# Attention as one written list of parts per pair, products with v in four visits, and the short chunk's scores in fp32 quarters

## The chip, the cores and the metric

One NeuronCore of a Trainium2 chip runs the whole program. The metric is device time in microseconds (us), the median of several runs; less is better. The engines are named as in the profile: PE (TensorE, with PEld its weight loads), DVE (VectorE), ACT (ScalarE), POOL (GpSimd) and SP, which issues the transfers.

## What is computed

Three layers, one behind the other. The attention has 4 batches of 8 heads, 576 tokens and a head size of 64:

```python
scores = scale * np.matmul(q, k.transpose(0, 1, 3, 2))
thresh = np.max(scores, axis=-1, keepdims=True) - tau
scores = np.where(scores >= thresh, scores, -1000000000.0)
scores = scores - np.max(scores, axis=-1, keepdims=True)
attn = np.exp(scores)
attn = attn / (np.sum(attn, axis=-1, keepdims=True) + 1e-09)
return np.matmul(attn, v).astype(np.float32)
```

Its output, 2304 tokens of 512 values, goes through an MLP (512 to 2048 to 512, with h * tanh(softplus(h)) between), and that through a soft mixture of 8 experts with 4 slots each. Everything is fp32; only the attention is touched by the change, apart from the layout of the inputs.

## The kernel before, in words

Two heads of a batch make a **pair**; there are NPR = 16 pairs. A pair's queries are cut into **chunks** of 128 score rows: four chunks of 128 queries for each head, and one short chunk that holds the last 64 queries of both heads, nine in all. The line `chunks += ...` (L283) gives their order: queries 0 to 127 of head 0, then of head 1, and so on, the short chunk last.

Inputs are split so that matmuls in the reduced format fp32r (one matmul instruction) keep fp32's accuracy. k is scaled by -1/8 into `ks` (fp32); `kb` holds its high part on partitions 0 to 63 and the low part on 64 to 127 (`prep_k`, L220). q is split into `Q1` (high part, on both halves) and `Q2` (low part), L233. This is POOL's work, one pair ahead; the first pair is split by ACT, DVE and POOL (`prep_first`, L239). A product of two fp32 tiles, as those with v, shows as two matmul instructions in the profile.

A chunk passes through these steps:

- **S** (`emit_S`, L293): scores into a PSUM tile `s` of two banks, 288 keys in each; 4 matmuls. For the short chunk `Q1` and `Q2` have 64 zero columns, so that each head's 64 queries fill their own half of 128 rows: 10 matmuls of 128 columns by 288, 224 or 64.
- **E** (`emit_E`, L311): DVE takes the minimum `nm` (L316; the scores are negated), ACT the exponential `e` (L317). Then `th` = `nm` + tau (L323, DVE).
- **P** (`emit_P`, L326): DVE keeps `e` where the score is within the threshold, and sums the row (L339).
- **T** (`emit_T`, L345): PE transposes four blocks of 128 keys into a bank `tp`, and ACT copies them to `pT` (L362, L364; a copy by ACT is line L93 in the profile).
- **R** (`emit_R`, L366 on, and `evac_R`): the last 64 keys of both heads of a chunk are transposed together into the unused columns of an `s` tile and copied to `pTr`.
- **V** (`emit_V`, L389): the product with v, heads side by side in two 64-column halves of the array, in five steps over keys (four of 128 and the rest). The queries go in two halves, of 256 and of 320, each into one bank `tp`, which stays open over two visits: three steps, then two (`PV`, L36). ACT copies the result to `xT`.

PSUM has three `s` tiles (`ps_s`, six banks) and two `tp` banks (`ps_t`). A tile is written again only when its readers are done: S of a chunk waits for P of the chunk three before.

The order on every engine is the order in which the code emits. The loop at L558 goes over chunks i and emits in each turn: a visit of V if one is due, R, S of chunk i, another V, T of chunk i-3 (`T_LAG`), minimum and exponential of chunk i, P of chunk i-1, the threshold of chunk i, and then the side work by j, the place in the pair: k of the next pair at j = 1 and 3, q at 5 and 7, loads of the pair after next at 4 and 8, steps of the conversion of early weights (`conv_w` with fine; `CONV`, L39), the norm of the batch before (`norm_c`, L444, POOL, at 5), and in pairs 12 to 15 the split of the first MLP block's x (`x_hi` on ACT, `x_lo` on POOL, L463, at 6). Nine more turns drain the last pair, with the first MLP products (`mm1`, L490 to L492) between.

What the prediction speaks of further: the first MLP stage's second product (L654 to L656), the transposed MLP (L749 to L751) and the logits (L801, four 32-column tiles of the array), none of which is changed.

Of the kernel before, what the change touches and what calls it, by code (L numbers as in the profile page):

```python
# [18 lines left out]
NP = H // 2  # L19
# [50 lines left out]
def kernel(  # L70
    ctx: ExitStack,
    tc: tile.TileContext,
    q: bass.AP,
    k: bass.AP,
# [55 lines left out]
    Q1 = [p1.tile([128, 2 * S + 64], F32R, name=f"Q1_{i}") for i in range(2)]  # L130
    Q2 = [p1.tile([128, 2 * S + 64], F32R, name=f"Q2_{i}") for i in range(2)]
# [73 lines left out]
    def load_first():  # L205
        kt = raw[0, "k"] = p1.tile([128, 2, S], F32, name="kr")
        qt = raw[0, "q"] = p1.tile([128, 2, S], F32, name="qr")
        for h in range(2):
            sp.dma_start(out=kt[:, h], in_=k[0, 0, :, h])
            sp.dma_start(out=qt[:, h], in_=q[0, 0, :, h])  # L210
# [18 lines left out]
    def q_parts(n, h):  # L229
        o = slice(0, S) if h == 0 else slice(S + 64, 2 * S + 64)  # L230
        return Q1[n % 2][:, o], Q2[n % 2][:, o]

# [6 lines left out]
    def prep_first():  # L239
# [4 lines left out]
        def part(x, h, c):  # L244
            return x[:, slice(S + 64 + c.start, S + 64 + c.stop) if h else c]
# [5 lines left out]
        def low_k(h):  # L251
            dve.tensor_tensor(out=kb[64:, h], in0=ks[64:, h], in1=kb[64:, h].bitcast(F32), op=ALU.subtract)
# [21 lines left out]
        low_q(1, z, pool)  # L274
# [7 lines left out]
    for n in range(NPR):  # L282
        chunks += [(n, c, h) for c in range(4) for h in range(2)] + [(n, 4, 0)]  # L283
# [3 lines left out]
    def q_off(c, h):  # L287
        return 128 * c + (S + 128 if h else 0)
# [3 lines left out]

    def emit_S(i):  # L293
        n, c, h = chunks[i]
        q1, q2 = Q1[n % 2], Q2[n % 2]
        kb = KB[n][0]
        s = st[i]["s"]
        whole = ((0, 0, SH, 0), (1, 0, SH, SH))
        if c < 4:
            plan = [(t, q_off(c, h), h, whole) for t in (q1, q2)]  # L300
        else:
            rot = ((0, 0, SH, 64), (1, 0, SH - 64, SH + 64), (1, SH - 64, SH, 0))
            plan = [(q1, 512, 0, whole), (q2, 512, 0, whole), (q1, S, 1, rot), (q2, S, 1, rot)]
        for j, (t, o, hh, parts) in enumerate(plan):
            for f, a, z, ko in parts:
                pe.matmul(  # L306
                    s[:, f, a:z], lhsT=t[:, o:o + 128], rhs=kb[:, hh, ko:ko + z - a],
                    start=(j == 0), stop=(j == len(plan) - 1 and z == SH),
                )

    def emit_E(i):  # L311
        d = st[i]
        s = d["s"][:, :, :SH]
        nm = p1.tile([128, 1], F32, name="nm", bufs=4)
        e = p2.tile([128, 2, SH], F32, name="e", bufs=3)
        dve.tensor_reduce(out=nm, in_=s, axis=AX.XY, op=ALU.min)  # L316
        act.activation(out=e, in_=s, func=ACTF.Exp, bias=nm[:, 0:1], scale=-1.0)  # L317
        d["nm"], d["e"] = nm, e

    def emit_th(i):  # L320
        d = st[i]
        th = p1.tile([128, 1], F32, name="th", bufs=4)
        dve.tensor_scalar(out=th, in0=d["nm"], scalar1=tau_eff[:, 0:1], scalar2=None, op0=ALU.add)  # L323
        d["th"] = th
# [19 lines left out]

    def emit_T(i):  # L345
        n, c, h = chunks[i]
        half = 0 if c < 2 else 1
        if (n, half) not in pT:
            w = 256 if half == 0 else 320
            pT[n, half] = (  # L350
                p1.tile([128, 4, 2, w], F32, name=f"pT{half}"),
                p1.tile([128, w], F32, name=f"pTr{half}"),
            )
        t = pT[n, half][0]
        p = st[i]["p"]
        ps = ps_t.tile([128, 512], F32, name="tp").rearrange("p (a b) -> p a b", a=4)
        for kc in range(4):
            ko = 128 * kc + (64 if h else 0)
            pe.transpose(ps[:, kc], p[:, ko:ko + 128], ident)  # L359
        if c < 4:  # L360
            o = (c % 2) * 128
            copy_act(t[:, :, h, o:o + 128], ps)  # L362
        else:
            copy_act(t[:, :, :, 256:320], ps.rearrange("p a (h q) -> p a h q", h=2))  # L364
# [3 lines left out]
    def emit_R(n, part, i):  # L368


        ps = rest[n, part] = st[i]["s"][:, :, SH:SH + 128]
        if part == 2:
            pe.transpose(ps[:, 0], pr[:, 512:640], ident)
            return
        for j in range(2):
            pe.transpose(ps[:, j], pp[n, 2 * part + j][:, 512:640], ident)

    def evac_R(n, part):
        ps = rest.pop((n, part))
        if part < 2:  # L380
            copy_act(pT[n, part][1][:, :256].rearrange("p (a b) -> p a b", a=2), ps)
        else:
            tr = pT[n, 1][1]
            copy_act(tr[:64, 256:320], ps[:64, 0, :64])
            copy_act(tr[64:, 256:320], ps[:64, 0, 64:])
# [3 lines left out]
    def emit_V(n, half, kcs):  # L389


        b, hp = divmod(n, NP)
        w = 256 if half == 0 else 320
        t, tr = pT[n, half]
# [9 lines left out]
        if kcs[-1] < 4:  # L404
            return
        for blk, x0, p0, ln in spans(b * S + 256 * half, w):
            copy_act(xT[blk][:, hp, x0:x0 + ln], pv[:, p0:p0 + ln])

    def pv_at(i, z):

        n, k = divmod(3 * i + z, 27)
        for half, plan in enumerate(PV):
            for back in range(2):
                if k + 27 * back in plan and 0 <= n - back < NPR:
                    emit_V(n - back, half, plan[k + 27 * back])
# [7 lines left out]
    def norm_b(b, i):  # L423
        o = SH if i < NCH else 0
        ps = st[i]["s"][:36, 0, o:o + 128]
        pe.transpose(ps, rinv[b], ident)
        return lambda: norm_out(b, ps)

    def norm_out(b, ps):
# [78 lines left out]
    with tc.manual_schedule():  # L508
        dve.tensor_copy(out=idr, in_=ident)
        sp.dma_start(out=tau_sb, in_=tau)  # L510
        load_first()
        load_v(0)
        load_k(1)
        load_q(1)
# [4 lines left out]
        zz = const.tile([128, 64], F32, name="zz")  # L519
        dve.memset(zz, 0.0)  # L520
        for t in Q1 + Q2:
            dve.tensor_copy(out=t[:, S:S + 64], in_=zz)
# [4 lines left out]
        prep_first()  # L527
# [30 lines left out]
        for i in range(NCH + 9):  # L558
            n, j = divmod(i, 9)
            live = i < NCH  # L560
            if live or j in R_AT[1:]:
                st[i] = {"s": ps_s.tile([128, 2, 512], F32, name="s")}
            R = None
            pv_at(i, 0)
            if n < NPR and j == R_AT[0]:
                R = (n, 0, i)
            if n >= 1 and j in R_AT[1:]:
# [812 lines left out]
```

## Time and profile before

| | |
|---|---|
| runs | 741.07, 739.01 and 739.6 us, median 739.6 |
| profiled execution, span from the first to the last instruction | 737.1 us |
| the profiled execution's own time | not given apart from its span; the median of the runs is 2.5 us above that span |
| mean granted clock of TensorE | 0.992 of 2.4 GHz |
| attention with its drain | about the first 282 us |
| instructions | 12728 |

The page is one profiled execution. A busy share is an average over stages with other limits, so each stage is read from its own windows. In the chain of waits a piece is time in which the end of the program hung on that line; where pieces of PE follow each other without a gap, PE alone sets the pace. A matmul's own duration is longer than its share of that chain, since matmuls overlap.

### The profile page before, as it was taken

To read this page: it belongs to the slowest core of one execution; us is meant where nothing else is said; L and a number is where in the kernel's file an instruction comes from. 1 tells how busy PE (TensorE), PEld (TensorE's weight loads), DVE (VectorE), ACT (ScalarE), POOL (GpSimd) and SP (SyncE) were. 2 spreads that over 40 slices of the span, in tenths; PEclk is the share of its full clock that TensorE was granted. 3 is DMA by queue.
4 is the path that set the end of the run, shared out by engine and by line. 5 is a ranking of instruction groups with operands and counts; after the bars stand their busy time and mean duration, and the time that the engine had idled before them with its cause. 6 is when DMAs were issued, how large, how long until landed. Compare 5 with 4: busy or idle time off the path is not lost.

```text
span 737.1 us, 12728 instructions
## 1 busy us (share of the span) xinstructions
PE 717.8 (97%) x4625; PEld 587.9 (80%) x4625; DVE 527.1 (72%) x1018; ACT 453.2 (61%) x880; POOL 391.3 (53%) x395
## 2 busy tenths in 40 slices
PE   7999999999999999999999899999999999999995
PEld 6777777777777778999899888878898888888443
DVE  7999999999998855656977756578866446754413
ACT  6887787787777875445554645566656556545213
POOL 5766677667768642333746644566755544544000
PEclk8999999999999999999999999999999999999998
DMA  7422533453313023334311000000006111359798
GB/s 242 148 84 86 187 100 99 145 167 109 99 62 132 23 75 115 114 123 149 128 58 45 20 1 1 1 1 0 1 12 238 58 59 58 124 215 364 259 397 305
DMA packets 45678, 84.85 MB, mean 115 GB/s; under 512 B 6048, under 2 KB 21040, under 8 KB 45616
## 3 DMA queue, kind: packets, MB, share of 16 engines
q1 hardware_dynamic: 45344, 83.88, 33.6%
q8 instruction: 36, 0.59, 0.3%
q14 instruction: 26, 0.21, 0.1%
q10 hardware_dynamic: 272, 0.16, 0.1%
HBM read 79.23 MB, written 4.79 MB: 114 GB/s over the span
## 4 chain that ended last, share of the span: by engine, by line
PE 86%; ACT 5%; DVE 4%; issue 2%; POOL 2%; DMA 1%; SPq 0%; ACTq 0%
PE tp L403 11%; PE s L306 10%; PE s L654 9%; PE s L656 8%; PE s L655 8%; PE tp L359 8%; PE tp L749 5%; PE tp L751 5%; PE tp L750 5%; PE tp L490 3%; PE tp L492 3%; PE tp L491 3%; PE hp L1202 2%; PE so L1234 2%; ACT big L93 1%
## 5 line engine op out<-in xcount | busy, mean ns | idle before, releaser
L306 PE MATMUL s<-kb,Q 128*128 128x288 f32 (+2 forms) x672 | 125.4, 314 | 4.1 <-POOL Q L237 1.2
L473 POOL TENSOR_TENSOR wo<-wr,wo 128x512 fp32r<-128x512 f32 x48 | 68.3, 1424 | 99.9 <-ACT wo L93 86.5
L316 DVE TENSOR_REDUCE nm<-s 128x1 f32<-128x576 f32 x144 | 108.1, 751 | 17.8 <-PE s L306 15.4
L654 PE MATMUL s<-wo,gg 128*128 128x512 f32 x288 | 115.4, 401 | 0.7 <-DVE big L664 0.7
L656 PE MATMUL s<-wo,gg 128*128 128x512 f32 x288 | 113.6, 394 | 0.0
L655 PE MATMUL s<-wo,gg 128*128 128x512 f32 x288 | 113.4, 394 | 0.0
L93 ACT ACTIVATE pT<-tp 128x512 f32<-128x512 f32 x144 | 86.6, 601 | 38.8 <-PE tp L359 36.0
L317 ACT ACTIVATE e<-s,nm 128x576 f32<-128x576 f32 x144 | 106.7, 741 | 5.7 <-DVE nm L316 5.5
L306 PEld LDWEIGHTS s<-kb,Q 128*128 128x128 f32 x672 | 95.3, 192 | 18.4 <-issue 6.5
L339 DVE SCALAR_TENSOR_TENSOR pab<-s,th,e 128x576 f32<-128x576 f32 x128 | 103.5, 808 | 0.3 <-ACT pTr L93 0.3
L359 PE MATMUL tp<-ident,pab 128*128 128x128 f32 x512 | 79.2, 278 | 0.0
L403 PE MATMUL tp<-pT,vt 128*64 128x320 f32 (+1 forms) x512 | 76.0, 418 | 0.4 <-ACT pT L93 0.4
L739 POOL TENSOR_TENSOR wi<-wr,wi 128x256 fp32r<-128x256 f32 x48 | 47.2, 985 | 40.0 <-ACT wi L93 40.0
L760 ACT ACTIVATE hs<-hs 128x384 f32<-128x384 f32 x64 | 33.4, 522 | 56.5 <-DVE hs L1038 35.8
L359 PEld LDWEIGHTS tp<-ident,pab 128*128 128x128 f32 x512 | 61.1, 141 | 7.8 <-ACT e L317 4.9
L739 POOL TENSOR_TENSOR wi<-ev,wi 128x256 fp32r<-128x256 f32 x64 | 52.5, 831 | 23.8 <-ACT wi L93 23.8
L656 PEld LDWEIGHTS s<-wo,gg 128*128 128x128 f32 x288 | 54.1, 188 | 12.5
L654 PEld LDWEIGHTS s<-wo,gg 128*128 128x128 f32 x288 | 54.2, 188 | 9.8 <-issue 1.8
L655 PEld LDWEIGHTS s<-wo,gg 128*128 128x128 f32 x288 | 54.4, 189 | 7.4 <-POOL wo L473 0.4
L763 DVE TENSOR_TENSOR gg<-hs,gg 128x384 fp32r<-128x384 f32 x64 | 54.5, 852 | 7.6 <-ACT gg L93 7.6
L93 ACT ACTIVATE wi<-wr 128x256 fp32r<-128x256 f32 (+1 forms) x63 | 29.3, 465 | 37.7 <-DVE wr L168 22.6
L403 PEld LDWEIGHTS tp<-pT,vt 128*64 128x64 f32 x512 | 31.1, 136 | 24.0 <-issue 9.7
(284 smaller groups left out, 1565.2 us busy)
## 6 DMA issues: line engine op xcount, KB each, us to landing
kr<-in_k SPq DMA_DIRECT2D x32, 288.0 KB, 3.1
qr<-in_q SPq DMA_DIRECT2D x32, 288.0 KB, 3.0
big<-in_w SPq DMA_DIRECT2D x15, 512.0 KB, 7.2
wr<-in_w SPq DMA_DIRECT2D x14, 512.0 KB, 3.5
big<-in_w_in SPq DMA_DIRECT2D x10, 512.0 KB, 4.8
big<-in_w_out SPq DMA_DIRECT2D x10, 512.0 KB, 5.0
wr<-in_w SPq DMA_DIRECT2D x13, 352.0 KB, 7.6
big<-in_w SPq DMA_DIRECT2D x13, 320.0 KB, 6.9
```

The lines of the kernel that those rows point to most:

```text
L93: act.activation(out=dst, in_=src, func=ACTF.Copy)
L306: pe.matmul(s[:, f, a:z], lhsT=t[:, o:o + 128], rhs=kb[:, hh, ko:ko + z - a], start=(j == 0), stop=(j == len(plan) - 1 and z == SH),)
L316: dve.tensor_reduce(out=nm, in_=s, axis=AX.XY, op=ALU.min)
L317: act.activation(out=e, in_=s, func=ACTF.Exp, bias=nm[:, 0:1], scale=-1.0)
L339: dve.scalar_tensor_tensor(out=p.rearrange("p (a b) -> p a b", a=2), in0=d["s"][:, :, :SH], scalar=d["th"][:, 0:1], in1=d["e"], op0=ALU.is ...
L359: pe.transpose(ps[:, kc], p[:, ko:ko + 128], ident)
L403: pe.matmul(pv[hs, :w], lhsT=lhsT, rhs=rhs, start=(kc == 0), stop=(kc == 4))
L473: pool.tensor_tensor(out=t[:, 1], in0=src, in1=t[:, 0].bitcast(F32), op=ALU.subtract)
L654: pe.matmul(ps, lhsT=hi[:, ts], rhs=w[:, 0], start=(m == 0), stop=False)
L655: pe.matmul(ps, lhsT=hi[:, ts], rhs=w[:, 1], start=False, stop=False)
L656: pe.matmul(ps, lhsT=lo[:, ts], rhs=w[:, 0], start=False, stop=(m == NF - 1))
L739: pool.tensor_tensor(out=lo, in0=src, in1=hi.bitcast(F32), op=ALU.subtract)
```

## The change

The turn-by-turn loop gives way to one list, `PLAN`, that is gone through once per pair (and once more to drain). Each word is a step and a chunk or group number; a word with ' belongs to the pair before. S, X (exponential), D (minimum), H (threshold), P, T, C (the copy behind T) go by chunk; R and Q (the copy behind R), V and Z (the copy behind V) by group of queries; M is the side work of a place j; N and O are the batch's turned norm and its copy. On each engine the words stand in that order.

The short chunk is now the pair's first. Queries are grouped for v as (short chunk and queries 0 to 127), 128 to 255, 256 to 383, 384 to 511: one visit each with all five steps, into its own bank, 192, 128, 128 and 128 columns wide, with `pT` and `pTr` split likewise. The short chunk's scores use unsplit q (a new input `qt` with the last 64 queries, loaded by one transfer per pair) and the scaled k in fp32: two heads in the two 64-column halves of the array, keys 0 to 287 on partitions 0 to 63 and 288 to 575 on 64 to 127 (for head 1 the keys are stored rotated by 64, hence the fifth product). `Q1`, `Q2` and the loads of q lose their last 64 queries and the zero columns. The first pair's k is loaded ahead of its q; the rest of its split is emitted at the first M.

```diff
-T_LAG = 3
-PV = ({30: (0, 1, 2), 34: (3, 4)}, {41: (0, 1, 2), 46: (3, 4)})
-R_AT = (8, 4, 3)
-NORM_AT = (0, 5)
+CHUNKS = ((4, 0), (0, 0), (0, 1), (1, 0), (1, 1), (2, 0), (2, 1), (3, 0), (3, 1))
+GROUPS = ((4, 0), (1,), (2,), (3,))
+TURN = (((4, 0), 5), ((1,), 7), ((2,), 9), ((3,), 11))
+VISITS = ((0, (0, 1, 2, 3, 4)), (1, (0, 1, 2, 3, 4)), (2, (0, 1, 2, 3, 4)), (3, (0, 1, 2, 3, 4)))
+PLAN = "P7' S0 V0' S1 D0 Q2' Z0' X0 T6' H8' P8' H0 M0 D1 P0 T7' H1 C6' X1 M1 C7' R3' S2 V1' S3 D2 Z1' P1 Q3' T8' H2 X2 C8' M2 D3 T0 S4 P2 C0 M3 H3 D4 V2' R0 X3 S5 Z2' T1 T2 X4 P3 H4 S6 M4 D5 C1 P4 N0 C2 M5 Q0 V3' H5 X5 Z3' D6 T3 P5 R1 X6 T4 H6 O0 C3 M6 P6 S7 C4 D7 Q1 X7 M7 H7 S8 T5 C5 D8 R2 M8 X8"
+NORM_TILE = 6
+NQ = 512
+TAIL = S - NQ
...
-    Q1 = [p1.tile([128, 2 * S + 64], F32R, name=f"Q1_{i}") for i in range(2)]
+    Q1 = [p1.tile([128, 2 * NQ], F32R, name=f"Q1_{i}") for i in range(2)]
...
-        t = raw[n, "q"] = p1.tile([128, 2, S], F32, name="qr")
+        t = raw[n, "q"] = p1.tile([128, 2, NQ], F32, name="qr")
...
+    def load_qt(n):
+        b, hp = divmod(n, NP)
+        QT[n] = p2.tile([128, 2, TAIL], F32, name="qt")
+        sp.dma_start(out=QT[n], in_=qt[b, hp])
...
-        a, z = slice(0, 192), slice(192, S)
+        a, z = slice(0, 128), slice(128, NQ)
         scale_k(0)
-        low_k(0)
+        scale_k(1)
+        low_k(0, dve)
         high_q(0, a)
         low_q(0, a, dve)
-        scale_k(1)
-        high_q(0, z)
-        low_k(1)
-        high_q(1, a)
-        low_q(1, a, pool)
-        high_q(1, z)
-        low_q(0, z, pool)
-        low_q(1, z, pool)
+
+        def rest():
+            low_k(1, pool)
+            high_q(1, a)
+            low_q(1, a, pool)
+            high_q(0, z)
+            low_q(0, z, pool)
+            high_q(1, z)
+            low_q(1, z, pool)
+
+        return rest
...
+        if c == 4:
+
+
+            ks = KB[n][1]
+            rot = TAIL + SH
+            tiles = ((0, 0, SH, 0, 0), (1, 0, SH, TAIL, 0), (0, 0, SH, SH, 1))
+            tiles += ((1, 0, S - rot, rot, 1), (1, S - rot, SH, 0, 1))
+            for hh, a, z, ko, f in tiles:
+                rows = slice(64 * f, 64 * f + 64)
+                pe.matmul(
+                    s[64 * hh:64 * hh + 64, f, a:z], lhsT=QT[n][rows, hh], rhs=ks[rows, hh, ko:ko + z - a],
+                    start=True, stop=True,
+                )
+            return
...
+            pT[n, g] = (
+                p1.tile([128, 4, 2, w], F32, name=f"pT{g}", bufs=1),
+                p1.tile([128, w], F32, name=f"pTr{g}", bufs=1),
+            )
...
+        g, kcs = VISITS[visit]
+        w = sum(width(c) for c in GROUPS[g])
+        t, tr = pT[n, g]
         vt, vrt = V[n]
         if kcs[0] == 0:
-            pvs[half] = ps_t.tile([128, 512], F32, name="tp")
-        pv = pvs[half]
+            pvs[n, g] = ps_t.tile([128, 512], F32, name="tp")
+        pv = pvs[n, g]
         for kc in kcs:
             for h in range(2):
                 hs = slice(64 * h, 64 * h + 64)
                 lhsT, rhs = (vt[:, kc, h], t[:, kc, h]) if kc < 4 else (vrt[:, h], tr)
                 pe.matmul(pv[hs, :w], lhsT=lhsT, rhs=rhs, start=(kc == 0), stop=(kc == 4))
...
-        load_first()
+        load_k(0)
+        load_qt(0)
+        load_q(0)
         load_v(0)
         load_k(1)
+        load_qt(1)
         load_q(1)
         load_v(1)
...
+        for n in range(NPR + 1):
+            for word in PLAN.split():
+                op, x, m = word[0], int(word[1]), n - word.count("'")
+                if op == "M":
+                    sides(n, x)
+                elif op in "NO":
+                    if n >= 1 and n % NP == 0:
+                        if op == "N":
+                            norm_b(n // NP - 1, 9 * n + NORM_TILE)
+                        else:
+                            norm_out(n // NP - 1)
+                elif 0 <= m < NPR:
+                    if op in by_chunk:
+                        by_chunk[op](9 * m + x)
+                    else:
+                        by_pair[op](m, x)
```

## Rows read from the trace of the kernel before

**Rows 1.** The page: busy time by engine, and the chain that ended last.
```profile
PE 717.8 (97%) x4625; PEld 587.9 (80%) x4625; DVE 527.1 (72%) x1018; ACT 453.2 (61%) x880; POOL 391.3 (53%) x395
...
PE 86%; ACT 5%; DVE 4%; issue 2%; POOL 2%; DMA 1%; SPq 0%; ACTq 0%
```

**Rows 2.** Table by windows, the steady attention: busy us, clock, DMA share, GB/s.
```profile
20.30:260.40 240.10, 238.59 (x1814) 183.67 (x1814) 223.04 (x553) 190.52 (x372) 165.40 (x164) 1.00 0.35 109
```

**Rows 3.** Chain of waits from 163 to 183 us: start, us, what.
```profile
164.82 1.16 PE s L306 x10
...
167.00 0.44 PE tp L359 x4
167.43 1.45 PE tp L403 x12
168.88 0.73 PE s L306 x4
...
170.05 0.54 PE s L306 x4
170.59 1.01 PE tp L403 x8
171.60 0.59 PE tp L359 x4
...
174.46 1.77 PE tp L403 x12
...
177.91 1.23 PE tp L403 x8
...
180.91 1.16 PE s L306 x10
```

**Rows 4.** Timeline of PE: the short chunk's scores of the first and last pair.
```profile
18.86 1.41 PE L306 MATMUL s<-kb,Q 128*128 128x288 f32 x10
...
263.69 1.40 PE L306 MATMUL s<-kb,Q 128*128 128x288 f32 x10
```

**Rows 5.** Chain of waits, the logits at 464 us.
```profile
464.86 1.44 PE tp L801 x32
```

**Rows 6.** Timeline of DVE in the first pair: start, us, operation.
```profile
10.82 0.75 DVE L316 TENSOR_REDUCE nm<-s 128x1 f32<-128x576 f32 x1
...
17.79 0.81 DVE L339 SCALAR_TENSOR_TENSOR pab<-s,th,e 128x576 f32<-128x576 f32 x1
...
19.32 0.81 DVE L339 SCALAR_TENSOR_TENSOR pab<-s,th,e 128x576 f32<-128x576 f32 x1
```

**Rows 7.** Table by windows, three single periods: PE, PEld, DVE, ACT, POOL busy us.
```profile
132.41:148.74 16.33, 16.33 (x126) 12.51 (x126) 16.21 (x40) 13.01 (x28) 11.74 (x11) 1.00 0.43 132
164.82:180.91 16.09, 16.09 (x125) 12.49 (x125) 15.03 (x39) 12.47 (x27) 12.02 (x12) 1.00 0.34 104
230.34:247.07 16.73, 16.34 (x125) 12.50 (x125) 14.34 (x37) 13.01 (x27) 13.24 (x13) 1.00 0.28 92
```

**Rows 8.** Groups of ACT by form, 20 to 262 us: busy us, mean ns, idle before.
```profile
L93 ACT ACTIVATE pTr<-s 64x64 f32<-64x64 f32 x30 | 6.4, 214 | 0.2
...
L157 ACT ACTIVATE big<-big 128x1024 f32<-128x1024 f32 x3 | 3.4, 1147 | 0.0
...
L93 ACT ACTIVATE big<-tp 128x128 f32<-128x128 f32 x4 | 1.1, 277 | 1.5 <-PE tp L403 1.5
```

**Rows 9.** Chain of waits from 214 to 219 us.
```profile
214.48 1.84 POOL big L463
...
217.04 1.42 POOL Q L237
...
218.51 0.53 PE s L306 x2
```

**Rows 10.** Timeline of ACT at the start: first work on each head's k.
```profile
4.16 0.78 ACT L249 ACTIVATE kb<-kr,kscale 128x576 fp32r<-128x576 f32 x1 [2.14 <-DMA kr<-in_k]
...
6.03 0.78 ACT L249 ACTIVATE kb<-kr,kscale 128x576 fp32r<-128x576 f32 x1 [0.71 <-DMA kr<-in_k]
```

**Rows 11.** The page: weight loads of the products with v.
```profile
L403 PEld LDWEIGHTS tp<-pT,vt 128*64 128x64 f32 x512 | 31.1, 136 | 24.0 <-issue 9.7
```

More of the change, by code (lines that the diff above doesn't have):

```diff
@@ L129 @@
     pr = p1.tile([128, 640], F32, name="pr")
-    Q1 = [p1.tile([128, 2 * S + 64], F32R, name=f"Q1_{i}") for i in range(2)]
-    Q2 = [p1.tile([128, 2 * S + 64], F32R, name=f"Q2_{i}") for i in range(2)]
+    Q1 = [p1.tile([128, 2 * NQ], F32R, name=f"Q1_{i}") for i in range(2)]
+    Q2 = [p1.tile([128, 2 * NQ], F32R, name=f"Q2_{i}") for i in range(2)]
     wr = {}
@@ L244, in part @@
         def part(x, h, c):
-            return x[:, slice(S + 64 + c.start, S + 64 + c.stop) if h else c]
+            return x[:, h * NQ + c.start:h * NQ + c.stop]
         def scale_k(h):
@@ L282 @@
     for n in range(NPR):
-        chunks += [(n, c, h) for c in range(4) for h in range(2)] + [(n, 4, 0)]
+        chunks += [(n, c, h) for c, h in CHUNKS]
     NCH = len(chunks)
@@ L299, in emit_S @@
[L299 to L305, printed above, removed]
+        s = score_tile(i)
+        if c == 4:
[10 more added lines that the diff above has]
+            return
@@ L306, in emit_S, with emit_D @@
+        o = q_off(c, h)
+        kb = KB[n][0]
+        for t in (Q1[n % 2], Q2[n % 2]):
+            for f in range(2):
                 pe.matmul(
-                    s[:, f, a:z], lhsT=t[:, o:o + 128], rhs=kb[:, hh, ko:ko + z - a],
-                    start=(j == 0), stop=(j == len(plan) - 1 and z == SH),
+                    s[:, f, :SH], lhsT=t[:, o:o + 128], rhs=kb[:, h, f * SH:(f + 1) * SH],
+                    start=(t is Q1[n % 2]), stop=(t is not Q1[n % 2]),
                 )
-    def emit_E(i):
+    def emit_D(i):
@@ L312, in emit_E @@
         d = st[i]
[L313 to L320, printed above, removed]
-        d = st[i]
-        th = p1.tile([128, 1], F32, name="th", bufs=4)
+        nm = d["nm"] = p1.tile([128, 1], F32, name="nm", bufs=4)
@@ L343, in emit_P, with width, turned @@
         d["p"] = p
+    def width(c):
+        return TAIL if c == 4 else 128
+    place = {}
+    for g, cs in enumerate(GROUPS):
+        for z, c in enumerate(cs):
+            place[c] = g, sum(width(x) for x in cs[:z])
+    def turned(n, c):
+        g = place[c][0]
+        if (n, g) not in pT:
+            w = sum(width(x) for x in GROUPS[g])
+            pT[n, g] = (
+                p1.tile([128, 4, 2, w], F32, name=f"pT{g}", bufs=1),
+                p1.tile([128, w], F32, name=f"pTr{g}", bufs=1),
+            )
+        return pT[n, g]
     def emit_T(i):
         n, c, h = chunks[i]
[L347 to L354, printed above, removed]
         p = st[i]["p"]
-        ps = ps_t.tile([128, 512], F32, name="tp").rearrange("p (a b) -> p a b", a=4)
+        ps = st[i]["t"] = ps_t.tile([128, 512], F32, name="tp").rearrange("p (a b) -> p a b", a=4)
         for kc in range(4):
@@ L403, in emit_V, with emit_Z @@
                 pe.matmul(pv[hs, :w], lhsT=lhsT, rhs=rhs, start=(kc == 0), stop=(kc == 4))
[L404 to L415, printed above, removed]
+    def emit_Z(n, g):
+        b, hp = divmod(n, NP)
+        pv = pvs.pop((n, g))
+        runs = []
+        for c in sorted(GROUPS[g]):
+            o, t0, ln = place[c][1], NQ if c == 4 else 128 * c, width(c)
+            if runs and runs[-1][1] + runs[-1][2] == t0 and runs[-1][0] + runs[-1][2] == o:
+                runs[-1][2] += ln
+            else:
+                runs.append([o, t0, ln])
+        for o, t0, ln in runs:
+            for blk, x0, p0, ln in spans(b * S + t0, ln):
+                copy_act(xT[blk][:, hp, x0:x0 + ln], pv[:, o + p0:o + p0 + ln])
     def norm_a(b):
@@ L607 @@
                 b, hp = divmod(m, NP)
-                if hp == NP - 1 and j == (NORM_AT[0] if n < NPR else 0):
+                if hp == NP - 1 and j == 0:
                     norm_a(b)
```

136 lines of the change are left out of this document (57 added, 79 removed).

## The prediction

> **What bounds the kernel now.** I read four views in turn. The page's engine table and chain say that TensorE (PE) is busy 97% of the span and that the chain that ended last is 86% PE [rows 1]; the attention's three PE lines (scores L306, transposes L359, products with v L403) lead it. The table by windows shows where: from 20.3 to 260.4 us PE is busy 238.59 of 240.10 us at the full granted clock, VectorE 223.04, ScalarE 190.52 [rows 2]. So 15 of the 16 pairs are bound by PE, with VectorE 7% behind. The chain of waits then gives PE's price list for one pair [rows 3]: from the short chunk's scores at 164.82 on, nothing but PE stands in it until the next pair's at 180.91, a period of 16.09 us. Last, the two ends of that stretch: the short chunk's ten score matmuls start at 18.86 us in the first pair and at 263.69 us in the last [rows 4], so 15 periods took 244.83 us; 15 x 16.09 is 241.35, and 3.5 us are waits on something else.
>
> **PE, part by part** (prices from [rows 3]). *Short chunk's scores.* Ten matmuls, 1.16 us, go. Five fp32 products come, on four quarters of the array: two heads by two halves of the keys, each half on 64 of the 128 contraction rows, 288 columns each (the fourth quarter as 224 + 64). What one costs shows in the v products, fp32 too, where two heads lie side by side: a visit of three steps takes 1.45 us and one of two steps 1.01, so a step at 256 columns is 0.44; at 320 it is 1.77 - 1.23 = 0.54. That is 1.7 ns per column for a step of two products. For 288 columns: 0.49 us if all four quarters run at once, 0.98 if only the two heads do, 1.96 if nothing overlaps. No row has operands on half the rows. I take 0.49: the v products, and the logits, whose four 32-column quarters need 1.44 us for 32 matmuls of 192 columns [rows 5], run every side-by-side tile that they have. The Trainium skill (TensorE: Matmul & The Clock Gate, Part 3) says that row and column tiles compose; by it the term would be the same 0.49, and no run here shows it for rows.
>
> *Products with v in four visits.* Columns stay 192 + 3 x 128 = 576 against 256 + 320, so at 1.7 ns a column nothing changes; but there are 20 steps for 10. A fixed part per step, fitted through 0.44 and 0.54, is at most 0.04 us: 0 to 0.4 us a pair. The logits, 1.44 less an entry of 0.13, give 0.33 per step of 192 columns, 1.7 ns a column again, so the fixed part is near zero: I take 0.05. Entering a visit costs 1.45 - 3 x 0.44 = 0.13; leaving it 0.19 (the scores behind it take 0.73, elsewhere 0.54) or 0.15 (transposes 0.59, elsewhere four at 0.44). There are four visits before and after, so no change, except that the short chunk's scores now stand ahead of the first visit, in another tile shape: one more switch, 0 to 0.35 us, taken as 0.15, the nearest row being one side of a visit. The skill (TensorEngine Tiling (Array Packing), Key Properties) says that a change of tiling mode drains the array; by that rule the 0.15 is due and 0 is not, and the 0.13 to 0.19 us at each side of a visit agree.
>
> *Sum on PE:* -1.16 + 0.49 + 0.15 + 0.05 = -0.47, a period of 15.62 us; over 15 periods -7.0.
>
> **Does anything else then bind?** VectorE's instructions stay the same in number: from one product p to the next are 19.32 - 17.79 = 1.53 us when it runs back to back [rows 6], 13.8 a pair. Weight conversion and norms come on top: one pair (40 instructions) has VectorE busy 16.21 of 16.33 us, another (39) 15.03 of 16.09 [rows 7]. ScalarE gets more: five copies out of v visits instead of two, six turned rests instead of four. At 0.277 for 128 columns and 0.214 for 64 x 64 [rows 8] five more copies are at most 1.3 us; less, as the old ones were wider: 0.85. So 12.47 becomes 13.3 of 15.6 us. I walked one pair of the new list with these durations, and PE never waits: T0 needs a bank that Z1 frees about 0.5 us before, V2 one that C8 frees 0.3 us before, S4 needs P1, done over 1 us before. The tightest loop is exp 7, P7, D0, P8, then S2 in P8's tile: some 0.4 us to spare. A conversion's rebase on ScalarE, 1.15 us [rows 8], stands between X4 and C1, and V3 is queued behind C1's bank: about 0.3 us in three pairs. VectorE's conversion steps stand before D5 and P6 and eat most of its slack of 1.8 us. I charge 0.1 us a pair, +1.5, bounds 0 and 0.45 (then the period is 16.1 and the gain in it is gone).
>
> *Waits that go.* Of the 3.5 us, 2.6 lie in the last four pairs (16.73 against 16.09 [rows 7]): there GpSimd's low part of x, 1.84 us, stands ahead of the second head's q with its 1.42, and scores wait for it until 218.51 [rows 9]. In the new list the first score that needs that q is S2, behind S0, V0, S1, T6, T7 and R3, some 3.9 us into the pair, where q is ready at about 3.2. I take all 2.6 away; kept, it would cost 2.6. GpSimd has a new wait: the scaled k has one buffer and S0 now reads it, so the next pair's k starts only behind S0; queued behind it on GpSimd are that pair's k, q and the norm. With 12.02 to 13.24 us of work [rows 7] in 15.6 nobody waits for it.
>
> *Start.* S0 needs only the scaled k of both heads and the small tail of q, no high and low parts. The second head's k came third and was used at 6.03, the first head's at 4.16 [rows 10]; as second transfer it should be there half way, about 5.1. I let all that follows move up by that 0.9: the third minimum from 10.82 [rows 6] to 9.9, bounds 0 and -1.7. From there VectorE sets the pace, 1.53 a chunk: the eighth minimum at 17.5, and the second pair's S0 waits for P6 just before it and starts near 18.4. Before, the matching point is the end of the ten matmuls, 18.86 + 1.41 = 20.2 [rows 4]: -1.8, bounds -0.5 and -2.5. The transfer of q's tail adds one issue per pair on SP's queue, which is in no chain here: 0; were it late, S0 of that pair would be.
>
> *End and rest.* After the last scores PE has the same transposes, v products and first MLP products as before; the MLP stages keep PE dense, so a shift passes through: 0, bounds +-1.5.
>
> **Sum.** -7.0 + 1.5 - 2.6 - 1.8 = -9.9 on the profiled span of 737.1, which gives 727.2; the median of the runs shown is 739.6, 2.5 above that span, and I carry the 2.5 along: 729.7, rounded to 729.5.
>
> **Rivals.** (1) *The in-order lists give half of it back.* For: VectorE at 16.21 of 16.33 us, ScalarE fuller; against: the walk above. Period 15.95 instead of 15.62: 729.7 + 15 x 0.33 = 734.6. (2) *Only the heads overlap in S0*: +0.49 x 15 = 7.4, 737. For: no row shows half-row operands. (3) *Nothing overlaps in S0: slower than before.* Place: PE between R2 and V0, 1.96 instead of 0.49 us: +1.47 x 15 = 22, 751.7. It decides from an S0 of about 1.15 us on, where 15 x 0.66 eats the 9.9. Against it: v products and logits overlap in fp32. (4) *Weight loads show.* A load of 64 columns takes 0.136 us [rows 11], a round of 128 columns 0.11 (a transpose, 0.44 / 4 [rows 3]). If each of 30 such rounds a pair waited for its load, 30 x 0.026 x 15 = +12: 742. Against: a transpose loads 128 columns and keeps 0.11. The skill (TensorE: Matmul & The Clock Gate, Part 3) says that loads overlap running matmuls only where the row group differs, which would ask for this; the trace disagrees, by those 0.11. (5) *The list does not do what it is for*, PE waits as much as it saves, and the old period stays: about 739.
>
> **Chances.** Forecast 0.53, (1) 0.20, (2) 0.09, (3) 0.06, (4) 0.05, (5) 0.07. About 0.3% (2.2 us) is what a measurement of this kernel can tell from no change. The forecast, (1) and half of (2) are faster: 0.78. The other half of (2) and most of (5): 0.10 within it. (3), (4) and the rest: 0.12 slower. The range takes the forecast's bounds downward (S0 with no switch, a start of -2.5, no new waits: about 723) and upward (1), (2) and (5): 723 to 739.
>
> **What would show it.** Right: the short chunk's scores start every 15.5 to 15.8 us, in groups of four matmuls, and take about 0.5 us; v visits take 1.1 and 1.7 us; no score waits for q on GpSimd behind 200 us; the third minimum starts before 10.2 us; PE is busy near 99% of the stretch. Wrong: PE idle before V2, V3 or T4, put down to ScalarE's copies; S0 of 1 us or more; a v visit of 128 columns over 1.4 us; a granted clock under 1.00 behind 20 us.

## The result and the profile after

The changed kernel takes 731.79 us (median of 4 runs, 731.58 to 732.82) against 740.05 for the kernel before beside it (4 runs, 739.01 to 741.07): a ratio of 0.9892, 95% interval 0.9878 to 0.9906. The forecast of 729.5 with its range of 723 to 739 holds it. The profiled span went from 737.1 to 730.0 us, 7.1 less where the working had 9.9 less.

The page of the kernel after answers to [rows 1]:

```profile
PE 711.4 (97%) x5265; PEld 608.5 (83%) x5265; DVE 524.1 (72%) x1012; ACT 457.7 (63%) x956; POOL 387.6 (53%) x396
...
PE 86%; ACT 6%; DVE 4%; issue 2%; DMA 1%; SPq 0%; ACTq 0%; DVEq 0%
```

PE is busy 6.4 us less, and GpSimd's 2% have left the chain: these were the waits for q behind the low part of x. The average says little more. The chain of waits of the kernel after, for one of the last pairs (start, us, what), answers to [rows 3]:

```profile
227.41 0.65 PE s L319 x4
228.07 1.78 PE tp L438 x20
229.84 0.72 PE s L328 x4
230.57 0.87 PE tp L391 x8
...
232.08 1.24 PE tp L438 x20
233.32 0.72 PE s L328 x4
...
242.97 0.65 PE s L319 x4
```

The short chunk's scores (L319) take 0.65 us where ten matmuls took 1.16, and nothing but PE stands between one such row and the next: a period of 15.56 us. The four visits of v take 1.78 + 3 x 1.24 = 5.50 against 1.45 + 1.01 + 1.77 + 1.23 = 5.46 before.

PE's timeline of the kernel after shows where the short chunk's scores start in the first, second and last pair, which answers to [rows 4], and the first matmul of the MLP:

```profile
5.55 0.74 PE L319 MATMUL s<-ks,qt 64*64 64x288 f32 x10
...
20.74 0.72 PE L319 MATMUL s<-ks,qt 64*64 64x288 f32 x10
...
242.90 0.72 PE L319 MATMUL s<-ks,qt 64*64 64x288 f32 x10
...
261.53 0.42 PE L529 MATMUL s<-big,wi 128*128 128x384 f32 x1
```

In order, the 14 periods from 20.74 to 242.90 are 16.04, 16.24, 15.94, 16.01, 15.98, 15.71, 15.75, 16.03, 16.00, 15.79, 15.75, 15.78, 15.59 and 15.55. Seven of them lie above the 15.5 to 15.8 that the forecast asked for. The short chunk stood last in a pair before and stands first now, so its end in the first pair before (18.86 + 1.41 = 20.27) is set against 20.74; the first MLP matmul came at 268.26 before. Three stretches then hold the whole difference:

| stretch | before | after | change | predicted |
|---|---|---|---|---|
| start, to that point | 20.27 | 20.74 | +0.5 | -1.8 |
| 15 pairs and the drain, to the first MLP matmul | 247.99 | 240.79 | -7.2 | -8.1 |
| the rest | 468.84 | 468.47 | -0.4 | 0 |

The table by windows of the kernel after (busy us of PE, PEld, DVE, ACT and POOL, granted clock, DMA share, GB/s) gives the steady stretch, an early pair (the third), one with the conversion's rebase, one with conversion and norm, a late one and the start; it answers to [rows 2, 7]:

```profile
20.74:261.53 240.79, 239.65 (x2477) 209.05 (x2477) 229.33 (x573) 202.51 (x459) 162.88 (x165) 1.00 0.36 110
36.78:53.02 16.24, 16.04 (x165) 13.80 (x164) 16.04 (x39) 12.96 (x29) 9.59 (x10) 1.00 0.31 95
84.97:100.95 15.98, 15.74 (x164) 13.77 (x163) 14.44 (x38) 13.71 (x31) 10.97 (x11) 1.00 0.52 158
132.41:148.44 16.03, 16.02 (x166) 13.81 (x165) 15.63 (x40) 13.15 (x31) 11.29 (x11) 1.00 0.47 144
227.34:242.90 15.56, 15.56 (x165) 13.78 (x164) 14.32 (x37) 13.49 (x30) 12.88 (x14) 1.00 0.34 98
5.55:20.74 15.19, 11.68 (x72) 10.21 (x71) 12.49 (x31) 9.62 (x20) 12.31 (x13) 0.78 0.73 241
```

PE is busy 99.5% of the steady stretch in any case. The single pairs show what that hides: VectorE is busy 16.04 of 16.24 us in the early one and 14.32 of 15.56 in the late one. The pair with the rebase is long too (15.98), but VectorE has room in it (14.44).

Two timelines of the kernel after, VectorE's and ScalarE's, show what became of the start, for [rows 6, 10]. Ahead of them stands ScalarE's first work on q in the kernel before:

```profile
4.95 0.36 ACT L93 ACTIVATE Q<-qr 128x192 fp32r<-128x192 f32 x1
```

```profile
7.18 0.31 ACT L98 ACTIVATE Q<-qr 128x128 fp32r<-128x128 f32 x1 [1.42 <-DMA qr<-in_q]
7.73 0.75 DVE L336 TENSOR_REDUCE nm<-s 128x1 f32<-128x576 f32 x1
...
9.16 1.12 ACT L98 ACTIVATE Q<-qr 128x128 fp32r<-128x128 f32 x3
10.98 0.76 DVE L336 TENSOR_REDUCE nm<-s 128x1 f32<-128x576 f32 x1 [0.73 <-PE s L328]
```

The first scores start at 5.55, but their minimum only at 7.73, behind the low part of q on VectorE. For that q has to land, and it now comes behind both heads' k: its first part lands at 7.16 us, where in the kernel before it landed at 4.93. The third minimum starts at 10.98 (before 10.82): its scores wait for the high part of q, which ScalarE does at 9.16 behind the first exponential. The granted clock is half, 1.2 GHz, from 8.66 to 15.48 us; PE stood idle 1.26 us ahead of the second scores and 1.20 ahead of the third, from 8.4 us on. Before, it was half from 7.94 to 14.77, for as long.

### The profile page after: what moved, and what is told of

Same layout as the page of the kernel before. It is cut to its first block, busy times and chain, and to the rows that moved or that the text cites. A ratio compares the mean times of both kernels' runs of the same rounds, so it can differ in the third digit from the quotient of the medians.

```text
span 730.0 us, 14081 instructions
## 1 busy us (share of the span) xinstructions
PE 711.4 (97%) x5265; PEld 608.5 (83%) x5265; DVE 524.1 (72%) x1012; ACT 457.7 (63%) x956; POOL 387.6 (53%) x396
## 4 chain that ended last, share of the span: by engine, by line
PE 86%; ACT 6%; DVE 4%; issue 2%; DMA 1%; SPq 0%; ACTq 0%; DVEq 0%
PE tp L438 11%; PE s L328 9%; PE s L684 9%; PE s L686 8%; PE s L685 8%; PE tp L391 8%; PE tp L779 5%; PE tp L781 5%; PE tp L780 5%; PE tp L529 3%; PE tp L531 3%; PE tp L530 3%; PE hp L1232 2%; PE so L1264 2%; PE s L410 1%
## 5 line engine op out<-in xcount | busy, mean ns | idle before, releaser
L328 PE MATMUL s<-kb,Q 128*128 128x288 f32 x512 | 98.2, 320 | 3.3 <-ACT Q L98 2.5
L98 ACT ACTIVATE pT<-tp 128x512 f32<-128x512 f32 x144 | 81.7, 600 | 6.3 <-PE tp L391 5.5
L328 PEld LDWEIGHTS s<-kb,Q 128*128 128x128 f32 x512 | 73.7, 193 | 10.9 <-issue 4.3
L438 PE MATMUL tp<-pT,vt 128*64 128x128 f32 (+1 forms) x1024 | 76.9, 292 | 0.7 <-ACT pT L98 0.7
L391 PE MATMUL tp<-ident,pab 128*128 128x128 f32 x512 | 72.8, 275 | 0.4 <-ACT big L98 0.4
L438 PEld LDWEIGHTS tp<-pT,vt 128*64 128x64 f32 x1024 | 57.9, 136 | 12.2 <-issue 5.4
L391 PEld LDWEIGHTS tp<-ident,pab 128*128 128x128 f32 x512 | 58.8, 140 | 5.2 <-issue 1.7
```

What stands on the lines that cost most here:

```text
L98: act.activation(out=dst, in_=src, func=ACTF.Copy)
L328: pe.matmul(s[:, f, :SH], lhsT=t[:, o:o + 128], rhs=kb[:, h, f * SH:(f + 1) * SH], start=(t is Q1[n % 2]), stop=(t is not Q1[n % 2]),)
L438: pe.matmul(pv[hs, :w], lhsT=lhsT, rhs=rhs, start=(kc == 0), stop=(kc == 4))
```

## Experiments

Times without another name stand against 731.79 us for the kernel after; ratios are to the kernel before on the same chip (739.5 to 740.3). Line numbers are those of the kernel after.

**1. The short chunk's scores twice.**

```diff
-            for hh, a, z, ko, f in tiles:
+            for hh, a, z, ko, f in tiles + tiles:
```

> The changed kernel, with the short chunk's five products issued twice over (the second time writes the same scores again), so the short chunk's scores cost PE 0.49 us more in each of 16 pairs. Theory (PE sets the pace, and the four quarters are what made the period shorter): +0.49 x 16 = 7.8 us, less what of the 4.4 us of waits that are left in the pairs hides behind the longer scores: +4 to +8, about 738. Rival (the order of the list made the gain, and VectorE or ScalarE set the pace by now): +2 or less, under 734.

739.04 us, ratio 0.9989 (0.9979 to 0.9998). The chain of waits of this kernel:

```profile
103.18 1.15 PE s L319 x8
104.32 1.78 PE tp L438 x20
```

The second set costs 0.50 us (1.15 - 0.65), so the first is 0.50 of products and 0.15 of a switch. The best period rises from 15.55 to 16.07, and the whole by 7.25 us, 0.48 for each of 15 pairs. Thirteen of the 14 periods rise by 0.40 to 0.52, and the one from 132.41 us on by 0.17: PE sets the pace, and what is put on it is paid almost in full.

**2. All quarters on the same 64 rows.** k lies on both halves of the partitions, so the result stays the same.

```diff
-                rows = slice(64 * f, 64 * f + 64)
+                rows = slice(0, 64)
```

> The changed kernel, with both halves of the keys of the short chunk on partitions 0 to 63, so that only the two heads can lie side by side. Theory (the two row halves overlap in the changed kernel): the ten matmuls start in pairs, in two sets one behind the other, the scores take 1.14 us with the switch instead of 0.65, and the time rises as with the products issued twice, +4 to +8 us. Rival (row halves do not overlap, what starts together is held back inside the array): no change in the 0.65 and none in the time.

737.91 us, ratio 0.9971 (0.9960 to 0.9982). Its chain of waits:

```profile
86.67 1.12 PE s L319 x8
87.79 1.78 PE tp L438 x20
```

1.12 less the 0.15 is 0.97: twice the 0.50 of four quarters at once. So halves of the rows do run side by side in the changed kernel; in its records, the four quarters' first matmuls start at 20.736, 20.742, 20.749 and 20.756 us; in this one they start in pairs, at 20.689 and 20.696, then at 20.983 and 20.989. The Trainium skill (TensorE: Matmul & The Clock Gate, Part 3) says that row and column tiles compose; the trace agrees, by 0.50 us against 0.97. Without this overlap the change would bring 2 us instead of 8.

**3. v in two visits by queries.** Two groups (short chunk and queries 0 to 255; 256 to 511), all five steps each, in place of four.

```diff
-GROUPS = ((4, 0), (1,), (2,), (3,))
+GROUPS = ((4, 0, 1), (2, 3))
-VISITS = ((0, (0, 1, 2, 3, 4)), (1, (0, 1, 2, 3, 4)), (2, (0, 1, 2, 3, 4)), (3, (0, 1, 2, 3, 4)))
+VISITS = ((0, (0, 1, 2, 3, 4)), (1, (0, 1, 2, 3, 4)))
...
```

(The list loses its words V0', Z0', V2' and Z2', and V1', Z1', V3', Z3' become V0', Z0', V1', Z1'.)

> The changed kernel, with two visits to the products with v, of 320 and 256 queries and five steps each, at the places of the second and the fourth. Theory (a visit costs about 0.35 us to enter and leave whatever its width): PE's own work falls by 0.7 us a pair to 14.85; VectorE needs 13.8 and the conversion, so the period ends near 15.2: -3 to -7 us, about 727. Rival (a visit of 3.0 us leaves VectorE without scores, since only three score tiles exist): VectorE idles about 1 us behind each visit and the period is 16 or more: +2 to +8 us.

755.36 us, ratio 1.0206 (1.0191 to 1.0221), though PE has two entries less. PE's timeline and the waits from 40 to 240 us of this kernel (us in total, times, longest):

```profile
161.03 0.78 PE L328 MATMUL s<-kb,Q 128*128 128x288 f32 x4 [1.34 <-DVE pab L361]
...
163.44 2.37 PE L438 MATMUL tp<-pT,vt 128*64 128x320 f32 x16
...
171.81 1.52 PE L438 MATMUL tp<-pT,vt 128*64 128x256 f32 x12 [0.76 <-ACT pT L98]
```

```profile
PE s L328 <- DVE pab L361: 15.1, 12, 1.6
...
DVE nm L336 <- PE s L328: 14.4, 12, 1.4
```

A visit of 2.84 us in one piece (pieces of 2.37 and 0.71 that overlap) is longer than the work that the score tiles hold for VectorE: it runs dry (14.4 us), and then PE waits for it (15.1). In the kernel after, in the same window, these two are 1.5 us for VectorE and not listed for PE. The four visits save nothing on PE; they keep VectorE fed. The list was not put in another order for two visits, so this is the price of two visits at these places; and the kernel before had four visits too, of two and three steps.

**4 and 5. The kernel before, with the low part of x two places later.**

```diff
                 if 11 <= m < 15 and j == 6:
                     x_hi(0, m - 11)
+                if 11 <= m < 15 and j == 8:
                     x_lo(0, m - 11, pool)
```

> The kernel before, with GpSimd's low part of x emitted behind the second head's q (place 8 instead of 6) in pairs 12 to 15. Theory (those pairs wait for q behind x on GpSimd, and the new order removed just that): the last four periods fall from 16.5 to 16.9 us to about 16.1 and the time by 2 to 2.6 us, to about 737.5. Rival (something else of these pairs makes them long): no change.

739.35 us, ratio 0.9984 (0.9972 to 0.9995). The last periods fell from 16.75, 16.73 and 16.87 to 16.12, 16.08 and 16.21: the wait was worth 1.9 us there, so it was real, as [rows 9] had it. The period ahead of these three, 16.48, which the prediction counts among the four, stayed at 16.47; no low part of x stands in it. But the first MLP matmul came only 1.24 us earlier, since two periods from 164 us on, ahead of every edited step, grew from 16.09 and 16.20 to 16.46 and 16.47. The same kernel once more:

> The kernel before with GpSimd's low part of x behind q, looked at again, since the granted clock fell to half for 3.4 us at 418 us in the first look. Theory (three of the last periods fall by 0.6 us and nothing is given back): first MLP matmul 1.9 us earlier than in the kernel before, and the time 1.5 to 2 us less where the clock holds. Rival (periods before them grow, as the two of 16.47 in the first look): 1.2 us earlier at the first MLP matmul, and under 1 us in the time.

737.98 us, ratio 0.9971 (0.9960 to 0.9982), the first MLP matmul at 266.96 (-1.3), and the two longer periods again. The timelines of GpSimd and VectorE show what happens at their start; first the kernel before, then this one:

```profile
175.92 1.98 POOL L237 TENSOR_TENSOR Q<-qr,Q 128x576 fp32r<-128x576 f32 x1
...
175.94 0.68 DVE L163 SCALAR_TENSOR_TENSOR big<-big 128x512 uint32<-128x512 uint32 x1
```

```profile
175.84 1.42 POOL L237 TENSOR_TENSOR Q<-qr,Q 128x576 fp32r<-128x576 f32 x1
...
175.87 1.93 DVE L163 SCALAR_TENSOR_TENSOR big<-big 128x512 uint32<-128x512 uint32 x1
```

Two instructions start within 0.03 us of each other. One runs at its bare duration (0.68 for the conversion step, 1.42 for GpSimd's q), the other takes both together (1.98 or 1.93). Which of them wins differs between the two kernels, though nothing was edited up to there; where VectorE loses 1.25 us, the period is 0.37 longer. This toss is the likely cause of 0.37 of the 0.65 us given back, though no run set it apart. The period behind it grew by the other 0.28: in its chain of waits PE stands until 183.00 us for the next conversion step, a minimum and a product on VectorE, which was still late. In the kernel before nothing but PE stands there.

**6. The conversion's rebase at M0 instead of M4.**

```diff
-CONV = (4, 6, 13, 15, 22, 24, 31)
+CONV = (0, 6, 13, 15, 22, 24, 31)
```

> The changed kernel, with the conversion's first step (ScalarE's rebase, 1.16 us, three times in all) at the place 0 of its pair instead of 4. Theory (at place 4 it stands between the exponential of chunk 4 and the copy that frees the bank of the third and fourth visit to v, and PE waits about 0.3 us for each): pairs 1, 5 and 9 lose 0.3 us each and the fourth visit starts at 11.6 instead of 11.9 us in them: -0.6 to -1 us. Rival (ScalarE has no slack at place 0 either, so the wait moves): 0.

732.24 us, ratio 0.9902 (0.9889 to 0.9914): no gain. First the chain of waits of the kernel after, at the rebase (L162), then of this one:

```profile
93.08 1.27 PE tp L438 x20
...
95.17 1.16 ACT big L162
96.33 0.50 ACT pT L98
...
96.87 1.31 PE tp L438 x20
```

```profile
88.48 0.67 ACT big L162
...
89.38 0.63 ACT pT L98
...
90.05 1.31 PE tp L438 x20
```

In the kernel after the fourth visit waits for ScalarE's copy behind the rebase, at 11.8 us into the pair (96.87 - 85.04) against 11.6 in a pair without (239.00 - 227.41). At M0 the second visit waits instead, at 5.4 us against 4.7, and the three pairs take 16.51, 16.41 and 16.41 us for 16.04, 15.98 and 16.00: +1.3. In this kernel's profiled execution the second pair started 0.84 us earlier, by the clock at the start, which hides most of it. A place that looks free on ScalarE was not free for what stood behind it.

**7. The short chunk's scores, minimum and exponential ahead of q's split in the first pair.**

```diff
+            words = PLAN.split()
+            if n == 0:
+                for f in (emit_S, emit_D, emit_X):
+                    f(0)
+                first_q()
+                words = [x for x in words if x not in ("S0", "D0", "X0")]
...
```

(`first_q` holds the first high and low part of q of head 0.)

> The changed kernel, with the first pair's short chunk brought through scores, minimum and exponential ahead of the split of q, on VectorE's and ScalarE's queues. Theory (the first minimum waits at 7.73 us behind q's low part, which waits for q's landing at 7.16, and the third at 10.98 behind the exponential of the first): first minimum near 6.4, third 0.5 to 1.2 us earlier, the time 0.5 to 1 us less. Rival (from the third minimum on the first pair is paced by ScalarE and VectorE whatever the start): the second pair's first scores stay at 20.7 us and the time stays.

732.33 us, ratio 0.9899 (0.9887 to 0.9912): no change. The minimum comes earlier, but the start pair takes 15.24 us against 15.19, with the clock at half from 9.37 to 16.2 us. The order of the first minimum was not what held the start.

**8 and 9. One more conversion step of the middle kind (L168, twice) per half, in both kernels.** The step can be repeated without a change of the result.

```diff
-            return [rebase] + [lambda f=f, c=c: f(c) for c in halves for f in (shift, low_bits, sign)]
+            return [rebase] + [lambda f=f, c=c: f(c) for c in halves for f in (shift, low_bits, lambda c: (low_bits(c), sign(c)))]
```

> The changed kernel, with one step of the early weights' conversion done twice (an OR of the same bits, no other result): six more VectorE instructions of 0.94 us, 5.6 us in all, in pairs 2 to 4, 6 to 8 and 10 to 12. Theory (VectorE's slack is used up in the pairs with conversion, so it is PE's next limit): +2 to +5 us. Rival (PE alone sets the pace, VectorE has 1.2 us of slack in these pairs): under +1.

736.42 us, ratio 0.9957 (0.9945 to 0.9969): 4.6 more. The first three pairs that got a step take 16.93, 16.71 and 16.44 us for 16.24, 16.01 and 15.71, each 0.7 more. The other three take 1.65, 0.72 and 0.56 more; in the one with 1.65, the step behind the added one met GpSimd's low part of q and took 1.65 us for 0.69. Together the 14 periods are 5.1 longer.

> The kernel before, with the same six VectorE instructions more. Theory (its period is 0.5 us longer, so VectorE has that more to spare): less than in the changed kernel, 0 to +2 us. Rival (slack of VectorE has nothing to do with the waits that are left): the same as in the changed kernel.

743.68 us, ratio 1.0051 (1.0036 to 1.0067): 4.2 more. My theory, that the old kernel with its longer period on PE would hide most of it (0 to 2 us more), falls. That it hides some is left: in the profiled execution its 15 periods are 3.2 longer, and the first MLP matmul comes 3.0 later. The rest came behind the attention, where the granted clock was half from 423 to 427 us, as it was not in the kernel before. In pairs with conversion VectorE is at or near its limit in both kernels.

**10. Three filler matmuls ahead of the second, third and fourth step of PE in the first pair.**

```diff
             for word in PLAN.split():
+                if n == 0 and word in ("S1", "S2", "T0"):
+                    warm(ps_t.tile([128, 512], F32, name="tp"), 3)
```

> The changed kernel, with three matmuls of 512 columns into an unused bank ahead of the scores of chunks 1 and 2 and of the first transposes of the first pair, where PE idles 1.2, 1.2 and 1.0 us. They write nothing that is read. Theory (PE's granted clock falls to half at 8.7 us because of these idle times and makes scores and transposes of the first pair twice as long until 15.5 us): the clock stays at full, the second pair's first scores start at about 19.7 instead of 20.74 us, as in the run of this case whose clock happened to hold there, and the time is 0.7 to 1.1 us less. Rival (VectorE and ScalarE pace the first pair, or the added matmuls delay the scores behind them as much): 0 to +1 us.

730.82 us (730.66 to 731.03), ratio 0.9868 (0.9855 to 0.9882): the best version. Its window of the start pair, and PE's timeline to the second pair's first scores:

```profile
5.50:19.75 14.25, 12.41 (x81) 9.53 (x80) 12.46 (x32) 9.68 (x20) 11.46 (x12) 1.00 0.71 230
```

```profile
18.43 0.80 PE L328 MATMUL s<-kb,Q 128*128 128x288 f32 x4 [0.42 <-DVE pab L361]
19.06 0.60 PE L391 MATMUL tp<-ident,pab 128*128 128x128 f32 x4
19.50 0.32 PE L410 MATMUL s<-ident,pab 128*128 128x128 f32 x1
19.75 0.72 PE L319 MATMUL s<-ks,qt 64*64 64x288 f32 x10
```

The granted clock is 1.00 in place of 0.78, and the second pair starts at 19.75 in place of 20.74. The 1.0 us arrives at the end: the first MLP matmul at 260.61 for 261.53, the median 1.0 lower (the two intervals of the ratios just touch, and the profiles decide). That it is the clock, and not something else that the fillers do, experiment 8 shows by chance: in its profiled execution the clock was full at the start without fillers, although PE stood idle 1.16 and 1.20 us there, and its second pair's first scores came at 19.62. So the clock at the start differs from execution to execution (in that of experiment 6 it was half for 3.4 us only), and the idle times alone do not settle it. Half a clock over 6.8 us cost only this 1.0: VectorE was busy 6.09 of those 6.82 us in the kernel after.

**11 and 12. The threshold on the exponential, and the same with the fillers.** P compares e with exp(-tau) in place of the score with its minimum plus tau, so that P reads no PSUM and H is not needed. The comparison is decided on the exponential's rounding.

```diff
-            out=p.rearrange("p (a b) -> p a b", a=2), in0=d["s"][:, :, :SH], scalar=d["th"][:, 0:1], in1=d["e"],
-            op0=ALU.is_le, op1=ALU.mult, accum_out=rs[b][:, col:col + 1],
+            out=p.rearrange("p (a b) -> p a b", a=2), in0=d["e"], scalar=cut[:, 0:1], in1=d["e"],
+            op0=ALU.is_ge, op1=ALU.mult, accum_out=rs[b][:, col:col + 1],
```

> The changed kernel, with the threshold taken on the exponential (e at least exp(-tau)) instead of on the score, so that VectorE's threshold instruction goes, nine of 0.12 us of its queue in each pair, and a score tile is free behind the exponential; which scores lie within the threshold is then decided with the exponential's rounding. Theory (the 4.4 us of waits left in the pairs stand behind a VectorE queue that is late where the conversion adds to it): periods of all pairs fall to 15.55 to 15.65 us and the time by 2.5 to 4.5 us, to about 728. Rival (ScalarE's queue is what is late): under 1 us less. If the product's instruction is slower with both operands in SBUF, the time rises instead.

772.42 us, ratio 1.0430 (1.0415 to 1.0445). The timeline of VectorE and GpSimd in this kernel:

```profile
119.44 1.34 POOL L95 TENSOR_SCALAR kb<-kr,kscale 128x576 fp32r<-128x576 f32 x1
119.44 0.80 DVE L360 SCALAR_TENSOR_TENSOR pab<-e,cut 128x576 f32<-128x576 f32 x1
...
120.87 2.04 DVE L360 SCALAR_TENSOR_TENSOR pab<-e,cut 128x576 f32<-128x576 f32 x1
120.87 1.42 POOL L233 TENSOR_TENSOR kb<-ks,kb 64x576 fp32r<-64x576 f32 x1
```

P alone still takes 0.80 us. Where it meets a GpSimd operation, one of the two takes its own time and the other about the sum: 1.34 for GpSimd's scaling (0.75 elsewhere) beside P's 0.80, then 2.04 for P beside GpSimd's 1.42. P's mean goes from 812 to 1233 ns over 128 instructions. So the run tells nothing of what a VectorE with one instruction less would give; that stays open. With the fillers:

> The two edits before together. If they act on different places their gains add: about 727. If the first pair's pace is VectorE's, the two overlap and the gain is that of the larger.

772.31 us, ratio 1.0434 (1.0418 to 1.0451). The start pair is 0.8 shorter (16.78 us for 17.55), the second pair's first scores come 0.3 earlier, and the rest is as slow: the two gains do not add, since the first is none.

## Why the prediction was right, and where its terms were off

**PE's price list held.** Scores of 0.49 and a switch of 0.15 were 0.50 and 0.15 (experiments 1 and 2). The Trainium skill's rule that a change of tiling mode drains the array (TensorEngine Tiling (Array Packing), Key Properties) asked for the switch, and the 0.15 agrees. The visits came to 5.50 for 5.51 (5.46 + 0.05). The best period is 15.55 for 15.62: transposes that now stand in eights take 0.87, or 0.44 for four, where one group of four behind a visit took 0.59. That is part of the rest; the term is -0.54 x 15 = -8.1 for -7.0.

**Rivals 2 to 5 fall by the same rows.** Experiment 2 is rival 2 made real, at 737.9 us for its 737. Rival 4, weight loads that show, would have made a visit of 128 columns 0.13 + 10 x 0.136 = 1.49 us; it takes 1.24, which is 0.13 + 10 x 0.11. Rival 5, the old period, falls by the mean period of 15.87. The page's row for rival 4's loads is as in [rows 11], 136 ns:

```profile
L438 PEld LDWEIGHTS tp<-pT,vt 128*64 128x64 f32 x1024 | 57.9, 136 | 12.2 <-issue 5.4
```

**GpSimd's waits went as forecast.** The last two full periods are 15.59 and 15.55; with 16.73 before, the 0.64 above 16.09 is gone. The term of 2.6 was too large for them: 1.9 of it is GpSimd's (experiments 4 and 5). The rest belonged to the smaller waits, which went too.

**New waits were the step that was too small: "I charge 0.1 us a pair".** Over the 14 periods the sum above 15.55 is 222.2 - 217.7 = 4.5 us, 0.32 a pair; it lies inside the bounds of 0 and 0.45, but 3 us above the charge. The mean period, 15.87, is nearer to rival 1 (15.95) than to the forecast with its charge (15.72): that rival was half right, and PE's extra 0.07 a period and the smaller waits of before (0.9 us of the 3.5), which went too, cover for it. Experiments 8 and 9 show the mechanism for most of it: the nine pairs with steps of VectorE's conversion but without the rebase hold 3.1 of the 4.5 us, VectorE has next to no slack in them, and 0.7 us more on it costs about 0.7. PE has as little there: in the third pair 0.50 more on PE cost 0.45 (experiment 1) and a step of 0.68 more on VectorE cost 0.69, so the two wait for each other in turn. What I had not priced is that the conversion's steps don't have one duration. VectorE's and GpSimd's timelines of the kernel after, in the third and fourth pair:

```profile
46.48 1.28 POOL L242 TENSOR_TENSOR Q<-qr,Q 128x512 fp32r<-128x512 f32 x1
46.75 1.55 DVE L168 SCALAR_TENSOR_TENSOR big<-big 128x512 uint32<-128x512 uint32 x1
...
62.69 1.28 POOL L242 TENSOR_TENSOR Q<-qr,Q 128x512 fp32r<-128x512 f32 x1
63.03 1.22 DVE L165 TENSOR_SCALAR big<-big 128x512 uint32<-128x512 uint32 x1
```

Alone these steps take 0.68 and 0.42 us; behind GpSimd's low part of q they end about when that is done plus their own time. Summed over the 18 fine steps VectorE loses 3.8 us so, more than half of it in the third to fifth pair. In the kernel before the same count gives 5.6 us, beside a longer period on PE. The walk of one pair used bare durations and could not see it. The rebase ahead of V3 came as forecast, with 0.2 in three pairs (experiment 6). These three pairs are 0.43 to 0.49 above the best period each, 1.4 of the 4.5 us, although VectorE has room in them; the other half of it, behind V3, has no experiment. How the 4.5 us divide among all these causes was not measured one by one.

**The start had the wrong sign: "I let all that follows move up by that 0.9".** It took 20.74 for 18.4. Only the first scores moved up; the third minimum did not (10.98 for 9.9). Its scores need q, and the working left out that q was moved back behind both heads' k (7.16 us for 4.93), and that its part for the third chunk stands behind ScalarE's first exponential. An earlier head of a chain moves the rest only up to the next input that does not come earlier. Of the 2.3 us, 1.0 is the clock (experiment 10), which the kernel before had at half for as long; the order on VectorE was none of it (experiment 7). The other 1.35 can be read from the timeline with the fillers: the third minimum at 10.60 for 9.9 is 0.7; the end of P5, five chunks on, at 18.37, where the forecast's five chunks end at 17.5, has 0.2 more; and from there PE has S8, T5 and R2 ahead of the second pair's first scores (the rows of experiment 10), 1.4 us where the forecast took 0.9. No experiment set these three apart.

**The balance**, against -9.9: start +2.3, new waits +3.0, PE -1.1, the small waits of before -0.9, end -0.4. That is -7.0; the span shows -7.1. The total was good partly because errors of both signs met, and that part was luck.

## What to carry to other kernels

A price list taken from stretches of the chain in which only the bounding engine stands predicts that engine's part to a few hundredths of a microsecond; the second engine wants the same care, stretch by stretch, with the longest duration of each of its operations and not only the bare one. Where the first input of a stage is made to come earlier, name the next input that stays where it was, or that comes later for it. A product that keeps PE for longer than the score tiles can feed the other engine is better cut, even if PE pays entries for it.

## What the runs showed of the hardware that was not expected

- VectorE and GpSimd shut each other out for nearly whole instructions: 0.68 or 1.93 us for the same step (experiments 4 and 5); 0.80 or 2.04 for P, once both its inputs lie in SBUF (experiment 11). Where GpSimd starts 0.27 us ahead, VectorE loses (46.48 and 46.75 in the kernel after); within 0.03 us it goes either way. The Trainium skill (SBUF — State Buffer, SBUF: two separate sides) says that the port pair which these two share is an exclusive lock, held for the whole instruction by whichever starts first, against VectorE operations with two SBUF inputs or in a mode that uses both ports; the rows agree, with the one difference that the record that starts 0.02 us earlier can be the one that loses (175.92 and 175.94 in the kernel before).
- Four fp32 quarters of the array, on both halves of the rows and of the columns, run fully side by side: 0.50 us for four times 288 columns, and 0.15 for the switch.
- With filler products in the waits of the first pair the granted clock stayed at 2.4 GHz in the profiled execution, which is worth 1.0 us of 731.8, although VectorE was the busier engine there. Without them it was half for 6.8 us in the kernel after, for 3.4 in experiment 6 and not at all in experiment 8, with much the same waits on PE.
